# Mixer and MLP kernel: weight loads cut into fewer pieces, x8 to x10 moved in the load queue, tile groups and engine assignments redrawn

## Chip, cores and metric

The kernel runs on one core of a Trainium2 chip. The metric is the device time of one execution in microseconds (us), taken as the median of several runs. TensorE is called PE below, VectorE DVE, ScalarE ACT, GpSimd POOL and SyncE SP.

## What is computed

The input x has 2048 rows of 512 features in bf16. Two blocks follow each other, each with a residual addition. The first normalises the rows, multiplies by w1 (512 x 512), applies GELU, shifts the four quarters of the features by +1, -1, +2 and -2 rows, and multiplies by w2 (512 x 512). The second normalises again, multiplies by w3 (512 x 1792), applies GELU and multiplies by w4 (1792 x 512).

```python
h = _gelu(_layernorm(x, axis=-1) @ w1)
c = D // 4
g0 = jnp.pad(h[:, :, 0*c:1*c], ((0, 0), (1, 0), (0, 0)))[:, :S, :]
...
hs = jnp.concatenate([g0, g1, g2, g3], axis=-1) @ w2
x1 = x + hs
h2 = _gelu(_layernorm(x1, axis=-1) @ w3) @ w4
return x1 + h2
```

## The kernel before

**Tiles and stages.** The 2048 rows are 16 tiles of 128 rows. All weights and all of x stay in SBUF. A tile t goes through these steps, and their names are used below. A tile index q from 0 to 15 means layer 1 of tile q; q from 16 to 31 means layer 2 of tile q - 16.

- `dma_x` loads x rows (L369), `dma_w` loads weight chunks (L378). One load can cover several tiles or chunks.
- `ln` makes the statistics and the normalised rows xn. Statistics are made by DVE (`bnst`, `bnag`: L415, L417), or, for the indices in `STAT_ACT`, by ACT (`sum` L394, `ssq` L399) with small DVE operations (`mean`, `msq`, `vpe`). POOL computes `rstd` with a power (L422). The normalisation `norm` runs on DVE (L443), ACT (L452) or POOL (L455), as `NORM` says; on ACT and POOL it needs one more small value, `nmr`, from DVE or POOL (`NMR`). Tile 0 is only centred, in two halves (L433), and its `rstd` is applied in its GELU.
- The transposition of xn to xT is either a DMA transpose that SP issues (`tp`, L461) or four PE transposes (`sa`, `sb`, `ty` in the script, L488), with a copy out of PSUM by ACT, DVE or both (`EVAC`, L496).
- `up1` multiplies by w1 (L624; tile 0 alone in another layout, `rows0`, L526, with the transposition `th` back), `mix` by w2 with shifted rows (L664), `up2` by w3 (L624), `down` by w4 (L693). GELU runs on ACT (L639). DVE adds the residuals: `x1` (L671, L675) behind `mix`, `res` (L701) behind `down`. Then SP writes the rows out (L704).

`up1` and `up2` work on groups of 1, 2 or 4 tiles (`GROUPS`): a group of n tiles gives matmuls of 128n columns. `mix` of tile t needs h of the next tile's first two rows as well, and so the group that holds them. `up2` needs all of w3, `down` all of w4.

**What sets the order.** PE's order is written out in `SCRIPT`. SP's and ACT's load order is written out in `LOADS`: an item such as `x7-10` is one load, `w3p`, `w3q`, `w3r`, `w3s` are the four quarters of a weight, `a` and `b` its halves, a bare name the whole; `@act` lets ACT issue it. An entry such as `tp6` says at which place in SP's list the transpose of that index stands; for an index that PE transposes it has no effect. The order of all else is planned when the program is built: `Program.order` gives every operation a due time counted from the PE order, and `Program.place` runs a list of operations through estimated durations, taking on each engine the ready operation that is due first. The planned order is fixed in the program; each engine works through its own list in that order and waits on semaphores, one per engine and one per DMA. `DUE`, `BEGIN` and `BIAS` are parameters of this plan. `emit` puts the waits: an operation that needs several loads carries one wait for each.

PSUM has two banks that `mix`, `down` and `th` take in turn (`next_bank`) and three pairs of banks that transposes and `up` take in turn (`next_pair`).

**The start.** PE first runs warm-up matmuls on zeros (`warm:11`, L717). Then come the transposes of tiles 0, 1 and 2, `rows0` for tile 0, `up1` for tiles 1 to 5 one by one, `mix` 0 to 3, and between them the transposes of tiles 3 to 5 and of layer 2's tiles 16 and 17. Behind them starts `up2:0`, the w3 product of tiles 0 and 1. It is the first operation that reads w3.

Of the kernel before, what the change touches and what calls it, by code (L numbers as in the profile page):

```python
# [25 lines left out]
class Program:  # L26
# [2 lines left out]

    HOP = {"pe": 200.0, "dve": 155.0, "act": 220.0, "pool": 120.0, "sp": 70.0}  # L30
    LOOK = {"dve": 300.0, "act": 300.0}
    DUE = 198048.0
    BEGIN = {"sp": 30.0, "act": 560.0, "pe": 400.0, "dve": 150.0, "pool": 450.0}
    ENTRY = 1900.0
    COLD, RESTART = 4300.0, 800.0
    LAG = {"load": 750, "tp": 700}
# [15 lines left out]
    def order(self):  # L52
# [58 lines left out]
        assert seen == len(self.ops), "cycle"  # L111
        if self.DUE:

            topo, left = [], [len(d) for d in preds]
            stack = [i for i, n in enumerate(left) if n == 0]
            while stack:
                i = stack.pop()
                topo.append(i)
                for j in succs[i]:
                    left[j] -= 1  # L120
                    if left[j] == 0:
                        stack.append(j)
            due, t = {}, self.DUE
            for op in self.ops:
# [12 lines left out]
        for op in self.ops:  # L137
            op.prio += BIAS.get(op.name, 0.0)
            if op.first is not None:
# [11 lines left out]
    def place(self, succs, order_only):  # L151
# [4 lines left out]
        for op in self.ops:  # L156
            if npend[op.idx] == 0:
                cands[op.eng].append(op)
        free = dict(self.BEGIN)
        rings = {"sp": [], "act": []}  # L160
# [96 lines left out]
        self.seq = out  # L257
        return out

GROUPS = {1: (1, 1, 1, 1, 1, 1, 2, 4, 2, 2), 2: (2, 4, 4, 4, 2)}  # L260
NORM = {1: "act", 5: "act", 6: "pool", 7: "pool", 8: "act", 9: "act", 10: "act", 11: "pool", 13: "pool", 18: "pool", 20: "pool", 21: "pool", 24: "act", 27: "pool", 28: "pool", 29: "pool"}
EVAC = {0: "dve", 1: "both", 4: "both", 5: "both", 6: "dve", 7: "dve", 8: "both", 9: "both", 10: "dve", 11: "both", 15: "both", 17: "dve", 19: "both", 20: "dve", 21: "dve", 24: "both", 25: "both", 29: "dve", 30: "both", 31: "dve"}
STAT_ACT = (0, 6, 7, 8, 9, 12, 13, 18, 21, 22, 25, 27)
TAIL = (256, 128, 128)
NMR = {0: "pool", 2: "pool", 3: "pool", 4: "pool", 5: "pool", 6: "pool", 7: "pool", 8: "pool", 14: "pool", 16: "pool", 18: "pool", 22: "pool", 25: "pool", 26: "pool", 28: "pool", 31: "pool"}
NAT = (0,)
SPLIT = (0,)
CSPLIT = ()
HEV = {0: "dve", 1: "dve", 2: "dve", 4: "dve", 6: "dve"}
BIAS = {"msq0": -366.448}  # L270
LOADS = """
x1 x2 w1a w1s w1r x3 x4 w2b x0@act w2q w2p x5 x6 tp5 w3r w3s x7-10 tp4 w3p tp5 w3q w4q w4p tp16 x12 w4r x11
w4s tp7 x13-14 x15
"""
SCRIPT = """
warm:11 sa:0 sb:0 ty:1-2 ra:0 rb:0 up1:1 th:0 up1:2 mix:0 ty:3 mix:1 ty:4 up1:3-4 ty:5 mix:2 ty:16 mix:3
ty:17 up1:5 up2:0 mix:4 down:0 up1:6 down:1 up1:7 mix:5-6 up1:9 mix:10 mix:9 up1:8 mix:8 mix:7 up2:1 mix:11
mix:13 up2:2 mix:12 down:5 down:2-3 mix:15 up2:3 mix:14 down:6 down:13 down:9 up2:4 down:4 down:10 down:7
down:11 down:8 down:12 down:14-15
"""  # L280

def bass_standalone__mixer_s_mlp__prompt_kernel(nc, x, w1, w2, w3, w4, out):
# [3 lines left out]
    NT, DC, FC = S // P, D // P, F // P  # L286
    groups = {l: [(sum(GROUPS[l][:i]), n) for i, n in enumerate(GROUPS[l])] for l in GROUPS}
    NXN, NO, NPAIR, NOB, NJ = 16, 4, 3, 2, 4
# [8 lines left out]
    with ExitStack() as es:  # L297
# [87 lines left out]
        def ln(layer, t):  # L385
# [3 lines left out]
            col = lambda a: a[:, q : q + 1]  # L389
            if q in STAT_ACT:  # L390
                if layer == 1:
# [22 lines left out]
            else:  # L414
# [4 lines left out]
                       writes=[(("mv", q), 0), (("vpe", q), 0)], dur=75)  # L419
            var = vpe[:, q : q + 1] if q in STAT_ACT else mv[:, q, 1:2]  # L420
            pg.add("pool", f"rstd{q}",
                   lambda e: e.tensor_tensor(col(rstd), var, neghalf[:], ALU.pow),  # L422
                   reads=[(("vpe", q), 0), (("neghalf",), 0)], writes=[(("rstd", q), 0)], dur=470)
            how = NORM.get(q, "dve")
            dst = xn_buf[:, slot(q), :]
# [19 lines left out]
            else:  # L445
                eng = NMR.get(q, "dve")
                pg.add(eng, f"nmr{q}",
# [17 lines left out]
        def pe_transpose(t, q, pair):  # L465
            layer = 1 if q < NT else 2
            how = EVAC.get(q, "act")
            if pair:
# [104 lines left out]
        def h_transpose(t):  # L573
            g = group_of[1, t]
            how = HEV.get(t, "act")
            k = NAT.index(t)
# [71 lines left out]
        def mm_mix(t):  # L648
# [20 lines left out]
            wr = [(("x1", t), 0)]  # L669
            if NT + t in STAT_ACT:  # L670
                f = lambda e: e.scalar_tensor_tensor(x1_sb[:, t, :], dst, 1.0, x_sb[:, t, :], ALU.mult, ALU.add,  # L671
# [197 lines left out]
```

## Time and profile before

| what | value |
|---|---|
| median of 5 runs | 137.07 us (136.97 to 137.83) |
| the profiled execution's own time | 136.99 us |
| its span, first to last instruction | 135.2 us |
| granted PE clock | 1.000 |
| PE's first useful matmul | 4.77 us |
| DMA moved in the slices up to 17 us | 158 to 378 GB/s |
| loads: x 2 MB; w1, w2 0.5 MB each; w3, w4 1.75 MB each | 26 issues (25 on SP, 1 on ACT) |

All times inside the span are counted from its start. Two further things help in reading the profile. A wait for several semaphores is put down to the one that seems to have come last, so that a wait for a load can carry the name of a compute engine. And a matmul's shown length holds its way through the array; the distance from one start to the next is what it costs PE.

### The profile page before, as it was taken

To read this page: it belongs to the slowest core of one execution; us is meant where nothing else is said; L and a number is where in the kernel's file an instruction comes from. 1 tells how busy PE (TensorE), PEld (TensorE's weight loads), DVE (VectorE), ACT (ScalarE), POOL (GpSimd) and SP (SyncE) were. 2 spreads that over 40 slices of the span, in tenths; PEclk is the share of its full clock that TensorE was granted. 3 is DMA by queue.
4 is the path that set the end of the run, shared out by engine and by line. 5 is a ranking of instruction groups with operands and counts; after the bars stand their busy time and mean duration, and the time that the engine had idled before them with its cause. 6 is when DMAs were issued, how large, how long until landed. Compare 5 with 4: busy or idle time off the path is not lost.

```text
span 135.2 us, 2020 instructions
## 1 busy us (share of the span) xinstructions
PE 131.0 (97%) x779; PEld 71.7 (53%) x791; DVE 52.2 (39%) x143; ACT 57.5 (43%) x92; POOL 27.7 (20%) x60
## 2 busy tenths in 40 slices
PE   8999799999999999999999999999999999999994
PEld 3478588464466444444444444444446854444463
DVE  3889785784168820070005325002502202214222
ACT  6679889970675376655550003566000640000000
POOL 2434497259042310025003001000100000000000
DMA  5899999944543033001100311100030101111112
GB/s 158 290 305 378 378 346 204 161 66 95 112 121 63 19 79 76 0 0 39 39 5 0 78 39 39 39 0 0 4 81 18 59 0 39 39 44 39 39 39 78
DMA packets 21449, 12.19 MB, mean 90 GB/s; under 512 B 14016, under 2 KB 20928, under 8 KB 21440
## 3 DMA queue, kind: packets, MB, share of 16 engines
q1 hardware_dynamic: 20864, 11.80, 33.3%
q10 hardware_dynamic: 576, 0.26, 0.7%
q8 instruction: 6, 0.10, 0.3%
q14 instruction: 3, 0.02, 0.0%
HBM read 6.82 MB, written 2.10 MB: 66 GB/s over the span
## 4 chain that ended last, share of the span: by engine, by line
PE 84%; DMA 6%; SPq 3%; ACT 2%; DVE 1%; issue 1%; DVEq 0%
PE y_ps L624 41%; PE o_ps L693 36%; PE o_ps L664 8%; DMA x_sb<-in_x_dram 6%; SPq L378 2%; SPq L369 1%; ACT junk L399 1%; ACT junk L394 1%; DVE x_sb L671 1%; DVE x_sb L675 0%; ACT xnT L496 0%; DVE vpe L411 0%; DVE o_sb L701 0%; DVEq L818 0%
## 5 line engine op out<-in xcount | busy, mean ns | idle before, releaser
L624 PE MATMUL y_ps<-xnT,w_sb 128*128 128x512 bf16 (+2 forms) x420 | 63.6, 308 | 1.2 <-DVE x_sb L675 1.0
L624 PEld LDWEIGHTS y_ps<-xnT,w_sb 128*128 128x128 bf16 x424 | 38.3, 98 | 25.7 <-DVE x_sb L675 1.1
L693 PE MATMUL o_ps<-w_sb,h2T 128*128 128x512 bf16 (+2 forms) x248 | 48.9, 355 | 0.2
L639 ACT ACTIVATE h2T<-y_ps 128x1024 bf16<-128x1024 f32 (+1 forms) x29 | 28.6, 994 | 39.8 <-PE y_ps L624 39.6
L693 PEld LDWEIGHTS o_ps<-w_sb,h2T 128*128 128x128 bf16 x252 | 23.4, 98 | 24.9 <-issue 0.4
L701 DVE TENSOR_TENSOR o_sb<-o_ps,x_sb 128x512 bf16<-128x512 f32 (+2 forms) x18 | 11.3, 630 | 35.5 <-PE o_ps L693 30.5
L422 POOL TENSOR_TENSOR rstd<-mv,neghalf 128x1 f32<-128x1 f32 x20 | 11.2, 560 | 44.1 <-DVE mv L417 43.7
L675 DVE TENSOR_TENSOR x_sb<-o_ps,x_sb 128x512 bf16<-128x512 f32 x11 | 7.5, 684 | 22.1 <-PE o_ps L664 22.1
L664 PE MATMUL o_ps<-w_sb,hT 128*128 128x512 bf16 x60 | 14.9, 379 | 0.2
L415 DVE BATCH_NORM_STATS2 st<-x_sb 128x6 f32<-128x512 bf16 x20 | 13.6, 684 | 2.4 <-DMA x_sb<-in_x_dram 2.2
L422 POOL TENSOR_TENSOR rstd<-vpe,neghalf 128x1 f32<-128x1 f32 x12 | 6.6, 552 | 22.5 <-DVE vpe L411 17.7
L639 ACT ACTIVATE hT<-y_ps 128x512 bf16<-128x512 f32 (+1 forms) x10 | 8.1, 809 | 6.6 <-PE y_ps L624 6.4
L664 PEld LDWEIGHTS o_ps<-w_sb,hT 128*128 128x128 bf16 x64 | 6.1, 98 | 6.0
L399 ACT ACTIVATE junk<-x_sb 128x512 bf16<-128x512 bf16 x12 | 7.5, 624 | 2.7 <-DVE x_sb L671 2.6
L443 DVE TENSOR_SCALAR xn_buf<-x_sb,mv,rstd 128x512 bf16<-128x512 bf16 x15 | 6.6, 441 | 4.2 <-POOL rstd L422 3.2
L671 DVE SCALAR_TENSOR_TENSOR x_sb<-o_ps,x_sb 128x512 bf16<-128x512 f32 x5 | 3.4, 689 | 12.2 <-PE o_ps L664 12.2
L455 POOL TENSOR_SCALAR xn_buf<-x_sb,rstd,nmr 128x512 bf16<-128x512 bf16 x10 | 7.6, 768 | 1.0 <-DVE nmr L448 0.4
L452 ACT ACTIVATE xn_buf<-x_sb,nmr,rstd 128x512 bf16<-128x512 bf16 x6 | 4.8, 810 | 0.9 <-DVE mv L417 0.9
L717 PE MATMUL o_ps<-zeros 128*128 128x512 bf16 x11 | 4.3, 570 | 0.6 <-POOLq L854 0.6
L394 ACT ACTIVATE junk<-x_sb 128x512 bf16<-128x512 bf16 x7 | 4.4, 623 | 1.3 <-DMA x_sb<-in_x_dram 1.3
L417 DVE BATCH_NORM_AGGREGATE mv<-st 128x2 f32<-128x9 f32 x20 | 3.8, 191 | 0.3
L488 PE MATMUL y_ps<-ident,xn_buf 128*128 128x128 bf16 x32 | 3.0, 220 | 0.1
(34 smaller groups left out, 27.9 us busy)
## 6 DMA issues: line engine op xcount, KB each, us to landing
out_dram<-o_sb SPq DMA_DIRECT2D x15, 128.0 KB, 1.7
w_sb<-in_w_dram SPq DMA_DIRECT2D x4, 448.0 KB, 7.5
x_sb<-in_x_dram SPq DMA_DIRECT2D x9, 128.0 KB, 3.7
w_sb<-in_w_dram SPq DMA_DIRECT2D x2, 512.0 KB, 8.8
w_sb<-in_w_dram SPq DMA_DIRECT2D x2, 384.0 KB, 9.2
w_sb<-in_w_dram SPq DMA_DIRECT2D x2, 256.0 KB, 4.0
w_sb<-in_w_dram SPq DMA_DIRECT2D x4, 128.0 KB, 3.8
x_sb<-in_x_dram SPq DMA_DIRECT2D x1, 512.0 KB, 7.7
```

Source lines behind the costliest of these rows:

```text
L394: (lambda d: (lambda e: e.activation(d, src, ACT_F.Copy, scale=1.0 / D, accum_out=mv[:, q, 0:1])))(junk[:, b, :]),
L399: (lambda d: (lambda e: e.activation(d, src, ACT_F.Square, accum_out=sums[:, q, 1:2])))(junk[:, b, :]),
L415: pg.add("dve", f"bnst{q}", lambda e: e.bn_stats(st9[:, q, 0:6], src), reads=rs, writes=[(("st", q), 0)], dur=605)
L422: lambda e: e.tensor_tensor(col(rstd), var, neghalf[:], ALU.pow),
L443: lambda e: e.tensor_scalar(dst, src, mv[:, q, 0:1], rstd[:, q : q + 1], ALU.subtract, ALU.mult),
L455: f = lambda e: e.tensor_scalar(dst, src, rstd[:, q : q + 1], nmr[:, q : q + 1], ALU.mult, ALU.add)
L624: ins = e.matmul(y_ps[:, p, W * i : W * (i + 1)], wsb[:, dc, P * fc : P * (fc + 1)], src[:, dc, P * t0 : P * t0 + W], start=(dc == 0), sto ...
L639: (lambda d, s: (lambda e: e.activation(d, s, ACT_F.Gelu_apprx_tanh)))(dst, ysrc),
L664: ins = e.matmul(dst, hT[:, j, c0 : c0 + P], w2_sb[:, j, :], start=(j == 0), stop=(j == DC - 1))
L675: f = lambda e: e.tensor_tensor(x1_sb[:, t, :], dst, x_sb[:, t, :], ALU.add)
L693: ins = e.matmul(dst, h2T[:, fc, P * t : P * (t + 1)], w4_sb[:, fc, cs], start=(fc == 0), stop=(fc == FC - 1))
L701: (lambda d, c: (lambda e: e.tensor_tensor(o_sb[:, oi, c], d, x1_sb[:, t, c], ALU.add)))(dst, cs),
```

## The change

Loads. w1 comes in two halves (before: a half and two quarters), w2 in two halves (before: a half and two quarters), w3 in one load (before: four quarters), w4 in two halves (before: four quarters). x4 and x5 come as one load, x6 and x7 as one, x8 to x10 as one, x11 and x12 as one. x8 to x10 stand behind w4's first half; before, x7 to x10 stood between two halves of w3. `tp6` is issued ahead of x11 to x15.

Groups. Layer 1 has groups of tiles 0, 1, 2, 3, 4-5, 6, 7-10, 11-12, 13-14, 15 (before: 0, 1, 2, 3, 4, 5, 6-7, 8-11, 12-13, 14-15). Layer 2 has 0-1, 2-5, 6-9, 10-11, 12-15 (before: 0-1, 2-5, 6-9, 10-13, 14-15).

PE's order. Up to `up2:0` the same tiles are worked, with one warm-up matmul less and some transposes moved. From there on, `up1:5` (tile 6) and both downs of tiles 0 and 1 come before `mix:5`, and later `mix`, `up2` and `down` steps are in another order.

Engines. The centring of tile 0 moves from DVE to POOL, the norm of tile 1 from ACT to DVE, that of tile 3 from DVE to ACT, that of tile 5 from ACT to DVE, that of index 16 from DVE to POOL; other norms, statistics and PSUM copies move likewise. The plan's parameters change too, and with them the planned order on DVE, ACT and POOL.

```diff
-    DUE = 198048.0
-    BEGIN = {"sp": 30.0, "act": 560.0, "pe": 400.0, "dve": 150.0, "pool": 450.0}
+    DUE = 164483.0
+    BEGIN = {"sp": 30.0, "act": 150.0, "pe": 400.0, "dve": 150.0, "pool": 450.0}
...
-GROUPS = {1: (1, 1, 1, 1, 1, 1, 2, 4, 2, 2), 2: (2, 4, 4, 4, 2)}
-NORM = {1: "act", 5: "act", 6: "pool", 7: "pool", 8: "act", 9: "act", 10: "act", 11: "pool", 13: "pool", 18: "pool", 20: "pool", 21: "pool", 24: "act", 27: "pool", 28: "pool", 29: "pool"}
...
-STAT_ACT = (0, 6, 7, 8, 9, 12, 13, 18, 21, 22, 25, 27)
+GROUPS = {1: (1, 1, 1, 1, 2, 1, 4, 2, 2, 1), 2: (2, 4, 4, 2, 4)}
+NORM = {0: "pool", 3: "act", 7: "pool", 8: "act", 9: "pool", 10: "pool", 11: "pool", 12: "pool", 14: "act", 15: "act", 16: "pool", 18: "act", 19: "act", 24: "pool", 25: "act", 26: "pool", 27: "pool", 29: "pool", 30: "pool", 31: "act"}
...
+STAT_ACT = (0, 7, 9, 12, 13, 15, 18, 21, 25, 29, 30)
...
-HEV = {0: "dve", 1: "dve", 2: "dve", 4: "dve", 6: "dve"}
-BIAS = {"msq0": -366.448}
+HEV = {0: "dve", 4: "dve"}
+BIAS = {}
 LOADS = """
-x1 x2 w1a w1s w1r x3 x4 w2b x0@act w2q w2p x5 x6 tp5 w3r w3s x7-10 tp4 w3p tp5 w3q w4q w4p tp16 x12 w4r x11
-w4s tp7 x13-14 x15
+x1 x2 tp2 x0@act w1a w1b x3 x4-5 tp5 w2a w2b x6-7 w3 tp17 w4a x8-10 w4b tp6 x11-12 tp1 tp16 x13-15
 """
 SCRIPT = """
-warm:11 sa:0 sb:0 ty:1-2 ra:0 rb:0 up1:1 th:0 up1:2 mix:0 ty:3 mix:1 ty:4 up1:3-4 ty:5 mix:2 ty:16 mix:3
-ty:17 up1:5 up2:0 mix:4 down:0 up1:6 down:1 up1:7 mix:5-6 up1:9 mix:10 mix:9 up1:8 mix:8 mix:7 up2:1 mix:11
-mix:13 up2:2 mix:12 down:5 down:2-3 mix:15 up2:3 mix:14 down:6 down:13 down:9 up2:4 down:4 down:10 down:7
-down:11 down:8 down:12 down:14-15
+warm:10 sa:0 sb:0 ty:1 ra:0 rb:0 ty:2 up1:1 th:0 up1:2 mix:0 ty:3 ty:5 mix:1 ty:4 up1:3-4 ty:16 mix:2 ty:17
+mix:3 up2:0 mix:4 up1:5 down:1 down:0 mix:5 up1:6-7 mix:8 mix:6 up1:9 mix:9-10 up1:8 mix:7 mix:11 up2:1
+mix:13 mix:15 up2:3 down:5 mix:12 up2:2 mix:14 down:2 down:4 down:3 down:6-8 down:11 down:9 up2:4 down:10
+down:12-15
 """
```

`EVAC` (which engine copies a PE transpose out of PSUM) and `NMR` change too. Of the transposes that PE makes, 0 goes from DVE to ACT and DVE by halves, 2 from ACT to both, 5 from both to ACT, and 16 from ACT to DVE; 1, 3, 4 and 17 stay as they were.

## The prediction, made before the changed kernel ran

> **What bounds the kernel now.** I read the busy shares first, then the chain that ended last, the waits of TensorE (PE), three stretches of the span, and last the single DMA issues and instructions around the one gap.
>
> The shares (engine, busy us, share of the span, instructions):
> ```profile
> PE 131.0 (97%) x779; PEld 71.7 (53%) x791; DVE 52.2 (39%) x143; ACT 57.5 (43%) x92; POOL 27.7 (20%) x60
> ```
> PE is the bound; only its gaps and its start can be won. The stretches (from:to, length, busy us of each engine, clock, DMA share, GB/s) are: from PE's first useful matmul to its gap, the gap, and the rest.
> ```profile
> 4.77:16.20 11.43, 11.20 (x135) 8.43 (x135) 9.67 (x31) 9.48 (x24) 4.00 (x9) 1.00 1.01 346
> 16.20:17.17 0.97, 0.02 (x2) 0.03 (x2) 0.79 (x3) 0.97 (x4) 0.91 (x3) 1.00 1.09 353
> 17.17:133.40 116.23, 115.66 (x634) 61.71 (x644) 39.10 (x102) 44.52 (x63) 20.94 (x37) 1.00 0.26 60
> ```
> I count the third stretch by hand. PE's pitch is 216 ns for 512 columns (down0: 14 in 3.02 us), 109 ns for 256 (16 in 1.75), 59 ns for 128 (16 in 0.94) and 0.22 us for four transposes. Summed from 17.17 over the script, I reach 44.13 exactly where up2:1 starts and 133.3 at the end: **behind 17.17 nothing is left to win.** In the first stretch the sum is 11.03 us of 11.43, so 0.4 us are small waits. The large one is the gap:
> ```profile
> PE y_ps L624 <- DVE x_sb L675: 1.0, 1, 1.0
> ```
> ```profile
> 17.17 6.27 PE y_ps L624 x56
> ```
> The first line (waits) names DVE's x1 addition, the second (chain) the work behind the gap, up2:0. But up2:0 reads only xT of tiles 16 and 17, whose last copy out of PSUM (DVE, 15.45) ended at 15.86, and w3. So the named engine is not the cause. The issue of w3's second quarter (start, us) and its landing (last number, us after the start):
> ```profile
> 7.79 1.05 SPq L378 DMA_DIRECT2D w_sb<-in_w_dram  x1
> ```
> ```profile
> w_sb<-in_w_dram SPq DMA_DIRECT2D x1, 448.0 KB, 9.0
> ```
> 7.79 + 9.0 = 16.79: **the gap waits for w3's last quarter.** The remaining 0.35 us is the waiting itself: up2:0 carries six semaphore waits (four loads, ACT, DVE), 0.06 us each. PE's idle 0.38 us "issue" before down0 (also six) and 0.19 before rows0's second half (three) give the same price.
>
> **The change, part by part.**
> *PE work.* The same tiles are transposed by PE (0 to 5, 16, 17), and matmul counts by width agree. Ahead of up2:0, tiles 4 and 5 become one group of 256 columns (1.75 us in place of 2 x 0.94, -0.13); behind it tiles 6 and 15 become single groups where 6-7 was one (+0.13). Sum 0, but the end is then the start of up2:0 + 116.2 + 0.13, if no new wait appears.
> *w3's place in the queue.* Before, w3's last byte stands behind 4224 KB (x 0 to 10, w1, w2, w3), after behind 3840 KB, since x8 to x10 (384 KB) go behind w4's first half. The four-tile x load took 14.44 - 12.98 = 1.46 us of landing time per 512 KB, so 384 KB are 1.1 us: w3 lands at 16.79 - 1.1 = 15.7. Fewer, larger issues at the start might fill the engines earlier (DMA share 0.67 in us 3 to 4): 0 to 0.4 us better. [...]landings ran from 1.0 us behind the moved bytes (x6) to 2.0 (w3), so at worst 16.6. I take 15.7. Up2:0 then has two waits in place of six: 0.12 us, not 0.35. So w3 frees PE at about 15.8, and **the chain ahead of up2:0 becomes the limit.**
> *The start.* Tile 0's centring moves from DVE to POOL in halves. No 256-wide POOL row exists; POOL's 512-wide norm took 768 ns, its 128x1 TENSOR_SCALAR 262, so by the line between them 515 (ends 0.26, DVE's own time, and 0.77). Behind rstd1 (ends 4.04) the halves end at 4.55 and 5.07, where DVE ended at 4.57 and 4.75. Norm1 goes from ACT (5.22) to DVE, at 4.07. Here a rule speaks against the change: the Trainium skill, SBUF — State Buffer, section "Who interferes with whom", says that a DVE tensor_scalar in a two-port mode and a POOL instruction hold one port pair, and the later one waits for the whole of the other. The trace has one such meeting:
> ```profile
> 30.79 0.77 POOL L455 TENSOR_SCALAR xn_buf<-x_sb,rstd,nmr 128x512 bf16<-128x512 bf16 x1
> 30.84 0.87 DVE L443 TENSOR_SCALAR xn_buf<-x_sb,mv,rstd 128x512 bf16<-128x512 bf16 x1 [0.30 <-POOL rstd L422]
> ```
> DVE's 0.87 (median of that line: 0.41) ended 0.15 behind POOL. By the row norm1 ends 0.15 behind one half (4.70) or both (5.2); by the rule, with a whole DVE turn between the halves, the second half ends near 5.5 and its transposes start at 5.6. Without any meeting they start at 5.2. I take +0.25 (0 to 0.45).
> *Walking PE on.* With pitches from the trace (bn_stats 0.61, with its own aggregate behind it 0.72, DVE norm 0.33, 256-wide copy 0.19, x1 add 0.65, POOL rstd 0.55, nmr 0.26, GELU 0.60 and 1.02, ACT sum with readout 0.72, PE to DVE or ACT 0.2) and no meeting: rows0 ends 6.37, ty2, up1:1 at 6.60 (6.67 before), up1:2 7.77, mix0 8.75, ty3 9.6, ty5 9.83 (norm5 ready 9.54), mix1 10.05, ty4 10.98 (norm4 ends 10.83), up1:3 11.2, up1:4 12.14, ty16 13.89 (norm16 on POOL: 13.43), mix2 14.1, ty17 15.0 (norm17 14.43), mix3 15.2 (its GELU ends 15.09), up2:0 16.07. Most inputs are ready 0.05 to 0.5 us before PE asks, so the moves of norms, copies and statistics between DVE, ACT and POOL cost nothing here, and the cover is that thin. With +0.25 and 0.1 for touches, **up2:0 starts at 16.4** (16.1 to 16.9).
> *Queues passed.* w2b's landing (behind 1792 KB, as x5 before: 5.0 + 3.8 = 8.7) meets mix0 at 8.75 to 9.0. On ACT, sum7 stands ahead of the copies of ty3 and ty5 and waits for x6-7 (x6 at 9.2 before, now 128 KB more: 9.7); the copy for up1:3 ends at 11.0, PE asks at 11.2. In SP's queue w4b is issued by about 14, as 2.0 MB stay outstanding there; tp6 follows when norm6 is done (15.1), then x11 to x15, then tp7 to tp11.
> *Behind up2:0.* Before, tp6 landed at 18.42 + 4.7 = 23.1, 0.6 us behind w4's last quarter (14.40 + 8.1 = 22.5); here issue and landing of each in turn:
> ```profile
> 18.42 1.30 SPq L461 DMA_TRANSPOSE xnT<-xn_buf  x1
> ```
> ```profile
> xnT<-xn_buf SPq DMA_TRANSPOSE x1, 4.7
> ```
> ```profile
> 14.40 0.43 SPq L378 DMA_DIRECT2D w_sb<-in_w_dram  x1
> ```
> ```profile
> w_sb<-in_w_dram SPq DMA_DIRECT2D x1, 512.0 KB, 8.1
> ```
> After, w4 ends behind 6016 KB in place of 6272: about 21.9, tp6 22.5. Up1:5 (tile 6) is asked for at 16.4 + 6.13 + 0.86 = 23.4: 0.9 us of cover; down1 follows at 24.4. x8 to x10 land at about 19.2 (5120 KB; before, w4p at the same place: 9.6 + 9.8); sums, norms and the transposes of tiles 7 to 10 (SP takes 1.3 us each, 2.5 to land) end near 29, up1:6 starts at 31.2. tp21 lands near 41.5, up2:1 starts at 43.8. I cost these moves at nothing; later orders stand behind 3 us per down.
> *One warm-up matmul less.* It ends 4.3 in place of 4.5; transposes start at 4.7 as before. The Trainium skill, TensorE: Matmul & The Clock Gate, section "Part 1: The HAM clock gate", puts the full clock after about 3.4 us of sustained work. Warm-up weight loads here go from 0.43 apart to 0.31 at 4.03 to 4.34, so it comes under the tenth matmul: cost 0 by the row; if it slips past the now idle 0.3 us, by the rule up to 3.4 us at half rate, 1.7 us. I take 0.
>
> **Sum.** 17.17 - 16.4 = 0.77, less 0.13: 0.64 us. The profiled execution took 136.99 us (span 135.2 and 1.8 around it), 0.08 below the median of 137.07. 136.99 - 0.64 = 136.35, and with the median's 0.08, **136.4 us** (-0.5%). 0.5%, 0.69 us, is about what a measurement of this kernel can tell from no change.
>
> **The rivals.**
> *The gap is refilled ahead of up2:0* (31%): x6-7 lands at 10.5, so sum7 holds the copy for up1:3 until 11.8, 0.6 us late; or both POOL halves run late; or w3 lands at 16.6. Up2:0 starts at 16.8 to 17.2: about 136.9. For it: DVE was busy 9.67 of 11.43 us there, and covers are thin. Against: 384 KB are off w3's way.
> *The transpose of tile 6 lands late* (13%): it now stands directly behind 2.7 MB of w3, x8-10 and w4 in one queue. The price is us for us from 23.4; past a landing at 24.0 the gain is gone, past 24.8 it is slower by over 0.5%. At 25.0, 136.4 + 1.6 = 138.0. Against: 256 KB less stand before it than before.
> *The change doesn't do what it says* would be w3 landing no earlier (16.8): up2:0 at 16.9, 136.9, inside the first rival.
>
> **Chances.** Main case 56%: 136.0 to 136.8. Over 0.5% faster means under 136.38: most of the lower half and the walk without a meeting (136.1), 46%. Within 0.5%: 39%. Slower: 15%, the late transpose or a missed clock. The range runs from 135.9 to 137.5.
>
> **What would show it.** Right: up2:0 starts near 16.4 with under 0.3 us of wait; w3 lands by 16; transposes of tile 0's second half start at 5.2 to 5.6; from up2:0 to the end 116.3 us. Wrong: a PE wait before up1:5, up1:6 or up2:1, a weight load pitch of 0.43 beyond 4.3, or up1:3 held by ACT's copy of tile 3.

## The result and the profile after

The changed kernel takes **136.13 us** in the median (43 runs; the middle half lies from 136.07 to 136.16), the kernel before 136.97 us beside it (80 runs; the middle half from 136.50 to 137.46). The ratio is 0.9942 with a 95% interval of 0.9928 to 0.9956, so 0.58% faster. Not only the median moved: between the quartiles the runs of before are spread ten times as wide. Some runs of either kernel are slow ones, over 1.5% above its fastest (five of the changed kernel's, two of these at 200.06 and 233.68 us), and the ratios, their intervals and the spans given for experiments leave slow runs out, so that a ratio is not exactly the quotient of the two medians. The profiled execution of the changed kernel took 136.20 us, with a span of 134.9 us.

In the changed kernel every line number is one lower than before. First its busy shares:

```profile
PE 131.0 (97%) x777; PEld 71.5 (53%) x790; DVE 50.8 (38%) x134; ACT 57.6 (43%) x90; POOL 31.5 (23%) x70
```

PE's work is the same; POOL took over 3.8 us of work. The stretches show where the idle time lies now. They run from the span's start to PE's first useful matmul, from there to `up2:0`, and from `up2:0` to the end (columns as before):

```profile
0.00:5.16 5.16, 4.45 (x10) 1.34 (x10) 2.63 (x8) 2.82 (x6) 2.52 (x15) 1.00 0.56 176
5.16:16.85 11.69, 10.97 (x118) 8.12 (x121) 9.85 (x28) 7.71 (x16) 6.46 (x12) 1.00 1.07 376
16.85:133.10 116.25, 115.58 (x650) 62.05 (x659) 38.11 (x100) 47.10 (x68) 22.56 (x44) 1.00 0.26 59
```

Before, PE had 11.43 us of walk and a gap of 0.97 us up to `up2:0`; now it has a walk of 11.69 us and no gap, but it starts 0.39 us later (5.16 against 4.77). The last stretch is as long as it was. PE's only wait among useful work has changed its place:

```profile
PE y_ps L487 <- POOL xn_buf L432: 0.6, 1, 0.6
```

L487 is PE's transpose and L432 the centring of tile 0: PE waits once, for 0.6 us, for POOL's second half. No wait stands before `up2:0`, as the timeline of PE has it (start, length):

```profile
16.85 6.28 PE L623 MATMUL y_ps<-xnT,w_sb 128*128 128x256 bf16 x56
```

w3 had long been there. Its one load was issued at 4.52 us, and landed 9.3 us later, at 13.8 us (before: 16.8):

```profile
4.52 0.47 SPq L377 DMA_DIRECT2D w_sb<-in_w_dram  x1
```
```profile
w_sb<-in_w_dram SPq DMA_DIRECT2D x1, 1792.0 KB, 9.3
```

Landings differ from one execution to the next: eight others with w3 at this place of the list (a1, a3, c2, d1, g, g2, h1, h2 below) had it at 14.2 to 14.5 us, and with the list of before it was there at 16.4 to 16.8 (before, a2, a4). So the gap that bounded the start is gone by a margin of 2 to 3 us, and a new wait ahead of it gave back a part. The timeline of the changed kernel around that wait:

```profile
4.18 1.82 POOL L432 TENSOR_SCALAR xn_buf<-x_sb,mv 128x256 bf16<-128x256 bf16 x2
4.23 0.57 DVE L442 TENSOR_SCALAR xn_buf<-x_sb,mv,rstd 128x512 bf16<-128x512 bf16 x1
...
5.16 0.28 PE L487 MATMUL y_ps<-ident,xn_buf 128*128 128x128 bf16 x2
```

The two halves of the centring take POOL 1.82 us together, 0.92 each, and the transposes of the second half start at 6.06 us.

**The span and what lies around it.** Every run has a time and a span, and their difference is time that no trace shows. In the changed kernel it is 1.26 to 1.39 us in all of its runs. In the kernel before (67 runs beside the experiments b1, b2, c2 and g) it has two values: 1.27 to 1.38 us in 25 runs, 1.62 to 1.92 us in 42, and nothing between; the spans of the two sets are alike (medians 135.2 and 135.3). The median span of before is 135.1 to 135.4 us on the chips of the experiments, that of after 134.8 us in its own runs. So of the 0.84 us between the medians about 0.4 us are inside the span, and about 0.4 us (1.75 to 1.31) outside it. Only on the third chip of the experiments do both kernels have spans side by side: there 0.7 us are inside (135.4 to 134.7, h1), again with about 0.4 outside. The experiments are therefore read by both.

### The profile page after: what moved, and what is told of

It is laid out like the page before. It is cut to its first block, busy times and chain, and to the rows that moved or that the text cites. A ratio compares the mean times of both kernels' runs of the same rounds, so it can differ in the third digit from the quotient of the medians.

```text
span 134.9 us, 2004 instructions
## 1 busy us (share of the span) xinstructions
PE 131.0 (97%) x777; PEld 71.5 (53%) x790; DVE 50.8 (38%) x134; ACT 57.6 (43%) x90; POOL 31.5 (23%) x70
## 4 chain that ended last, share of the span: by engine, by line
PE 94%; DMA 2%; POOL 1%; issue 1%; DVE 1%; SPq 0%
PE y_ps L623 46%; PE o_ps L692 36%; PE o_ps L663 10%; DMA x_sb<-in_x_dram 2%; PE y_ps L487 1%; POOL xn_buf L432 1%; PE y_ps L525 1%; DVE st L414 1%; DVE o_sb L700 0%; PE o_ps L591 0%; DVE mv L416 0%; POOL rstd L421 0%; SPq L853 0%
## 5 line engine op out<-in xcount | busy, mean ns | idle before, releaser
L414 DVE BATCH_NORM_STATS2 st<-x_sb 128x6 f32<-128x512 bf16 x21 | 14.1, 678 | 2.8 <-DMA x_sb<-in_x_dram 2.6
L663 PE MATMUL o_ps<-w_sb,hT 128*128 128x512 bf16 x59 | 14.9, 379 | 0.3
L421 POOL TENSOR_TENSOR rstd<-vpe,neghalf 128x1 f32<-128x1 f32 x11 | 6.0, 549 | 28.5 <-DVE vpe L410 28.5
L454 POOL TENSOR_SCALAR xn_buf<-x_sb,rstd,nmr 128x512 bf16<-128x512 bf16 x11 | 8.4, 768 | 0.8 <-DVE nmr L447 0.4
L398 ACT ACTIVATE junk<-x_sb 128x512 bf16<-128x512 bf16 x11 | 6.9, 624 | 2.2 <-DVE x_sb L670 2.2
L442 DVE TENSOR_SCALAR xn_buf<-x_sb,mv,rstd 128x512 bf16<-128x512 bf16 x12 | 5.5, 455 | 2.8 <-POOL rstd L421 2.6
L451 ACT ACTIVATE xn_buf<-x_sb,nmr,rstd 128x512 bf16<-128x512 bf16 x8 | 6.3, 806 | 0.6 <-POOL nmr L447 0.6
L393 ACT ACTIVATE junk<-x_sb 128x512 bf16<-128x512 bf16 x6 | 3.7, 624 | 0.8 <-DMA x_sb<-in_x_dram 0.8
L487 PEld LDWEIGHTS y_ps<-ident,xn_buf 128*128 128x128 bf16 x32 | 2.1, 98 | 2.9 <-POOL xn_buf L432 1.8
```

Source lines behind the costliest of these rows:

```text
L398: (lambda d: (lambda e: e.activation(d, src, ACT_F.Square, accum_out=sums[:, q, 1:2])))(junk[:, b, :]),
L414: pg.add("dve", f"bnst{q}", lambda e: e.bn_stats(st9[:, q, 0:6], src), reads=rs, writes=[(("st", q), 0)], dur=605)
L442: lambda e: e.tensor_scalar(dst, src, mv[:, q, 0:1], rstd[:, q : q + 1], ALU.subtract, ALU.mult),
L451: f = lambda e: e.activation(dst, src, ACT_F.Identity, bias=nmr[:, q : q + 1], scale=rstd[:, q : q + 1])
L454: f = lambda e: e.tensor_scalar(dst, src, rstd[:, q : q + 1], nmr[:, q : q + 1], ALU.mult, ALU.add)
L663: ins = e.matmul(dst, hT[:, j, c0 : c0 + P], w2_sb[:, j, :], start=(j == 0), stop=(j == DC - 1))
```

## The experiments

My theory was the prediction's: w3 no longer holds PE, and the start holds it instead. The rival readings were that the load list alone makes the gain, that the groups and PE's order make it, or that the start costs nothing because it is absorbed further on. All medians stand beside runs of the kernel before on the same chip. The last two columns are medians too. An experiment has 6 to 22 runs (a2, a4 and g2 have 6).

| run | time | ratio to before | interval | span | around it |
|---|---|---|---|---|---|
| before, on three chips | 136.79 to 137.08 | 1 | | 135.1 to 135.4 | 1.68 to 1.75 |
| after | 136.13 | 0.9942 | 0.9928 to 0.9956 | 134.8 | 1.31 |
| a1: before, new loads | 137.38 | 1.0022 | 0.9999 to 1.0046 | 136.05 | 1.31 |
| a2: after, old loads | 138.00 | 1.0112 | 1.0073 to 1.0151 | 136.1 | 1.85 |
| a3: after, DVE centres | 135.84 | 0.9935 | 0.9913 to 0.9957 | 134.5 | 1.33 |
| a4: before, POOL centres | 137.96 | 1.0118 | 1.0070 to 1.0166 | 136.2 | 1.79 |
| b1: after, w3 in quarters | 136.10 | 0.9962 | 0.9943 to 0.9981 | 134.7 | 1.35 |
| b2: after, x8 to x10 early | 136.12 | 0.9945 | 0.9928 to 0.9962 | 134.8 | 1.32 |
| c2: before, new loads fitted | 136.46 | 0.9986 | 0.9962 to 1.0011 | 134.9 | 1.56 |
| g: after, POOL subtract and mult | 136.56 | 0.9998 | 0.9970 to 1.0026 | 135.2 | 1.31 |
| h1: after again | 136.05 | 0.9939 | 0.9914 to 0.9964 | 134.7 | 1.33 |
| h2: DVE centres again | 135.92 | 0.9923 | 0.9892 to 0.9953 | 134.6 | 1.31 |
| d1: DVE centres, ty3 before mix0 | 135.89 | 0.9900 | 0.9871 to 0.9930 | 134.6 | 1.31 |
| g2: POOL mult and add | 135.66 | 0.9902 | 0.9863 to 0.9941 | 134.3 | 1.31 |

a1 to a4 ran on one chip, b1, b2, c2 and g on a second, h1, h2, d1 and g2 on a third. Each edit makes the planner place everything anew, so some operations on DVE, ACT and POOL also change places: none in b1 and g2, a dozen in a3, some tens in a1, a2, b2 and c2.

### a1: the kernel before with the changed load list

```diff
-x1 x2 w1a w1s w1r x3 x4 w2b x0@act w2q w2p x5 x6 tp5 w3r w3s x7-10 tp4 w3p tp5 w3q w4q w4p tp16 x12 w4r x11
-w4s tp7 x13-14 x15
+x1 x2 tp2 x0@act w1a w1b x3 x4-5 tp5 w2a w2b x6-7 w3 tp17 w4a x8-10 w4b tp6 x11-12 tp1 tp16 x13-15
```

> The kernel before with the changed load list alone (groups, PE order and engine assignments stay; the plan's order on DVE, ACT, POOL and SP follows the new arrivals). Theory (the load order is what closed the gap): w3 lands near 14, up2:0 starts near 16.2 in place of 17.17, no wait before it, about 0.9 us faster, ratio 0.993. Rival (the gain is from the new PE order and engine assignments): ratio 0.998 or more.

It took 137.38 us: the time did not fall, and the span grew by 0.9 us. The gap at `up2:0` is gone (it starts near 16.7 us), and PE's waits show two others:

```profile
PE y_ps L623 <- issue: 1.2, 1, 1.2
PE o_ps L663 <- ACT hT L638: 0.8, 1, 0.8
```

The first stands before `up1:7`, the group of tiles 8 to 11. In the new list tile 11 comes with x12 behind w4's second half and lands at 22.2 us. The transposes of the four tiles then leave SP one after the other, the last two in this line (start, length, two issues), and a transpose needs 2.5 us to land:

```profile
29.01 2.58 SPq L460 DMA_TRANSPOSE xnT<-xn_buf  x2
```

The last is issued at 30.32 and lands at 32.8, where PE asks at 31.7. "issue" in the wait line thus hides a DMA. The second wait is before `mix:0`. The ACT operation that it names is the GELU of tile 2, which `mix:0` doesn't read and which ended at 9.52 us, when PE was already loading `mix:0`'s weights (9.41). w2's second half landed at 3.49 + 5.7 = 9.2 us. So the load list does remove the gap, but it brings two others. One comes from its fit to the old groups (tile 11). The other comes from the list itself: w2 was complete at 8.3 us in the profile of before and at 9.2 here.

### a2: the changed kernel with the load list of before

The diff is that of a1 with the signs exchanged.

> The changed kernel with the load list of before alone. Theory: w3's last quarter lands near 16.8 again and its six waits follow, up2:0 starts near 17.15 behind a gap of 0.3 us (PE is ready at 16.85), so about the time of before, ratio 1.000, and none of the 0.8 us that the start lost shows. Rival: the loads do not matter, ratio 0.994 as changed.

138.00 us: slower, not the same. PE's waits name tile 5's norm:

```profile
PE y_ps L488 <- DVE xn_buf L443: 0.9, 1, 0.9
```

The changed order asks for the transposes of tile 5 before those of tile 4. In the old list x5 stands alone behind w2 and lands at 8.6 us; DVE's timeline shows tile 5's statistics and its norm late behind it:

```profile
9.46 0.65 DVE L415 BATCH_NORM_STATS2 st<-x_sb 128x6 f32<-128x512 bf16 x1
...
11.42 0.40 DVE L443 TENSOR_SCALAR xn_buf<-x_sb,mv,rstd 128x512 bf16<-128x512 bf16 x1
```

`up2:0` starts at 18.22 us, though w3's last quarter was there at 16.4. Some 0.2 us of this belong to the profiled execution: PE was still at half its later pace until 6.6 us, and `up1:1` started at 7.71 (7.50 in the changed kernel). The rival that the new order is good by itself falls, as the rival that the new loads are good by themselves fell in a1. In span, each alone costs about 1.0 us, and both together save 0.3 to 0.7.

### c2: the kernel before with the new loads, fitted to its groups

a1's wait before `up1:7` comes from tile 11. So tile 11 goes with x8 to x10, as the old group of four wants it.

```diff
-x1 x2 tp2 x0@act w1a w1b x3 x4-5 tp5 w2a w2b x6-7 w3 tp17 w4a x8-10 w4b tp6 x11-12 tp1 tp16 x13-15
+x1 x2 tp2 x0@act w1a w1b x3 x4-5 tp5 w2a w2b x6-7 w3 tp17 w4a x8-11 w4b tp6 x12 tp1 tp16 x13-15
```

(the first line is a1's list)

> The kernel before with the changed load list, but x8 to x11 as one load and x12 alone, so that its group of tiles 8 to 11 has all its rows behind w4's first half. With the list as changed, that group waited 1.2 us for tile 11 before up1:7. Theory (loads and tile groups have to fit each other): that wait goes, up2:0 starts near 16.7 as there, ratio 0.994 to 0.997. Rival (the wait before up1:7 has another cause, such as the order of SP's transposes): it stays, ratio 1.002.

The wait is gone: `up1:7` starts without one, at 31.62, and of PE's waits among useful work only one of 0.3 us before `mix:0` is left.

```profile
31.62 3.62 PE L623 MATMUL y_ps<-xnT,w_sb 128*128 128x512 bf16 x15
```
```profile
PE o_ps L663 <- DVE mv L416: 0.3, 1, 0.3
```

Its median span, 134.9 us, is 0.25 us under that of before on the same chip (135.15) and within 0.2 us of b1's and b2's (134.7 and 134.8), which are the changed kernel but for a change in its loads. So by these medians a good half of the gain inside the span needs nothing but loads that fit, and the new groups, PE's new order and the engines add 0.1 to 0.2 us. In time c2 stays 0.3 us behind b1 and b2, since its time around the span is 1.56 us, not 1.32. Its ratio of 0.9986 misses the expected 0.994 to 0.997, and can't be told from no change.

### b1 and b2: which part of the load list brings w3 earlier

b1 gives the changed kernel w3 in four loads again, b2 puts x8 to x10 ahead of w3.

```diff
-... w2a w2b x6-7 w3 tp17 w4a x8-10 w4b ...
+... w2a w2b x6-7 w3r w3s w3p w3q tp17 w4a x8-10 w4b ...
```

> The changed kernel with w3 in four quarter loads at the same place of the list; all other order stays. In the profile of the changed kernel w3 landed at 13.8 and PE asked for it at 16.85. Theory (w3 now has some 3 us of slack; only the six waits of 0.06 us come back): last quarter lands by 15.8, up2:0 at 16.85 to 17.1, ratio 0.994 to 0.996. Rival (one load in place of four is what closed the gap): last quarter lands past 16.8, ratio 0.998 or more.

```diff
-... w2a w2b x6-7 w3 tp17 w4a x8-10 w4b ...
+... w2a w2b x6-7 x8-10 w3 tp17 w4a w4b ...
```

> The changed kernel with x8 to x10 ahead of w3 and not behind w4's first half. Theory: w3 lands 1.1 us later, near 15, still ahead of PE, so the move by itself is worth nothing while PE reaches up2:0 at 16.85: ratio 0.993 to 0.996, no wait before up2:0. Rival (the move is what closed the gap): a wait before up2:0, ratio 0.998 or more.

Neither moves the time (136.10 and 136.12 us). Issue and landing of the last quarter in b1:

```profile
6.13 0.43 SPq L377 DMA_DIRECT2D w_sb<-in_w_dram  x1
```
```profile
w_sb<-in_w_dram SPq DMA_DIRECT2D x1, 448.0 KB, 7.8
```

6.13 + 7.8 = 13.9 us, as the single load's 13.8: the number of w3's loads isn't what brought w3 forward. Nor did the waits for four loads, expected at 0.06 us each, cost anything that shows: the last matmul of `mix:3` started at 16.55 and `up2:0` at 16.76, one matmul's distance later. In b2, w3 as one load:

```profile
5.03 0.49 SPq L377 DMA_DIRECT2D w_sb<-in_w_dram  x1
```
```profile
w_sb<-in_w_dram SPq DMA_DIRECT2D x1, 1792.0 KB, 9.9
```

5.03 + 9.9 = 14.9 us. That is 1.1 us later than in the changed kernel's own profile, but only 0.4 to 0.8 us later than in the eight others. The prediction gave 1.1 us to 384 KB in the queue; at the 376 GB/s of the changed kernel's second stretch they are 1.05 us by estimate, and b2 agrees as far as one execution can tell. `up2:0` asks at 16.6, so even there w3 isn't late, and the move of x8 to x10 is worth nothing in this kernel. More than half of the 2 to 3 us comes from the rest of the list, since b2's w3 is still 1.5 to 1.9 us ahead of the 16.4 to 16.8 of the old list. By 13.5 us, 4.13 MB had been moved in the changed kernel against 3.82 MB before, which is 0.8 us of moving by estimate; the other part, how long w3 landed behind the moving of its bytes, was 2.0 us before and 0.9 to 1.8 in the executions of the changed list. Why was not isolated.

### a3 and a4: who centres tile 0

```diff
-NORM = {0: "pool", 3: "act", 7: "pool", ...
+NORM = {3: "act", 7: "pool", ...
```

> The changed kernel with tile 0's centring back on DVE alone. POOL took 0.92 us for each half where 0.515 was estimated. Theory (that delay lies on PE's path all the way to up2:0): the second half's transposes start near 4.9 in place of 6.06, up2:0 near 16.1 in place of 16.85, 0.7 us faster than the changed kernel, ratio to before 0.989. Rival (the delay is absorbed, as other inputs of the walk are late anyway): under 0.2 us, ratio 0.993 to 0.994.

```diff
-NORM = {1: "act", 5: "act", 6: "pool", ...
+NORM = {0: "pool", 1: "act", 5: "act", 6: "pool", ...
```

> The kernel before with tile 0's centring on POOL alone. Theory: the start comes 0.8 us later, but PE waits for w3 until 17.17 anyway, so up2:0 starts at 17.2 and the time stays, ratio 1.000 (at most 1.002). Rival (a late start shifts the end by itself): 0.8 us slower, ratio 1.006.

With DVE centring (a3), PE's transposes run on without a wait from 4.71 us and `up1:1` starts at 6.74 in place of 7.50. Then PE waits before `mix:0`:

```profile
PE o_ps L663 <- DVE st L414: 0.6, 1, 0.6
```

`mix:0` doesn't read those statistics. It reads h of tiles 0 and 1, which was complete at 8.60 us, and w2, whose second half landed at 3.48 + 5.6 = 9.1; `mix:0` started at 9.50. Of 0.76 us won at the start, 0.36 were left at `up2:0` (16.49 against 16.85), and 0.3 in the median span. The expected ratio of 0.989 was missed; 0.9935 is what the rival gave. In a4, POOL's centring costs the kernel before 1.2 us of waits, as its source line and PE's waits show:

```profile
L433 POOL TENSOR_SCALAR xn_buf<-x_sb,mv x2: 917/920/924, 5.2 to 6.1; 128x256 bf16<-128x256 bf16 x2
```
```profile
PE y_ps L488 <- POOL xn_buf L433: 1.2, 2, 0.6
```

Here POOL began at 5.2, behind another `rstd` in its list, `up1:1` started 1.8 us late, and `up2:0` about 1.0 us late: `up1:5`, directly before it, started at 17.2 us, and `up2:0` at 18.2. I had expected w3's gap to absorb all of it; the delay was larger than the gap. So a late start is absorbed only as far as the next load's landing lies behind it.

### g and g2: the price of POOL's centring

The sum of the prediction took 0.515 us for one half, and the trace has 0.92. Two runs change only the form of the operation, and g2 leaves every other operation in its place. g subtracts the mean and multiplies by 1. g2 lets ACT make the negative mean of tile 0 and has POOL multiply by 1 and add it; the values are the same.

```diff
-tensor_scalar(a, b, mv[:, q, 0:1], None, ALU.subtract)
+tensor_scalar(a, b, mv[:, q, 0:1], 1.0, ALU.subtract, ALU.mult)
```

> The changed kernel with tile 0's centring still on POOL in halves, but as subtract and multiply by 1.0 in one instruction, the shape of operations that POOL's other norms have. Same result. Theory (the instruction with one operation is slow on POOL by itself, 0.92 us for 256 columns against 0.77 for 512 with two): a half takes about 0.5 us, the second half's transposes start near 5.3, but w2's landing near 9.1 takes most of it back: ratio 0.9935 to 0.994. Rival (DVE, holding the shared port, or the narrower tile makes it slow): it stays at 0.92.

```diff
-activation(d, src, ACT_F.Copy, scale=1.0 / D,
+activation(d, src, ACT_F.Copy, scale=(-1.0 if q == 0 else 1.0) / D,
...
-tensor_scalar(a, b, mv[:, q, 0:1], None, ALU.subtract)
+tensor_scalar(a, b, 1.0, mv[:, q, 0:1], ALU.mult, ALU.add)
```

> The changed kernel with tile 0's mean kept with the other sign (ACT's scale is negative for tile 0), so that POOL's centring is a multiplication by 1.0 and an addition in place of a subtraction. Same result. Theory (subtracting is what is slow on POOL: 0.92 us alone and 1.14 with a multiplication, against 0.77 us for twice the columns with multiply and add): a half takes 0.5 us, its transposes start near 5.3, ratio 0.992. Rival (the half-wide tile is what is slow): 0.9 us or more, ratio 0.994 or above.

The source line of the centring in g, then in g2 (shortest, median and longest in ns):

```profile
L432 POOL TENSOR_SCALAR xn_buf<-x_sb,mv x2: 1140/1142/1145, 4.1 to 5.2; 128x256 bf16<-128x256 bf16 x2
```
```profile
L432 POOL TENSOR_SCALAR xn_buf<-x_sb,mv x2: 479/490/500, 3.9 to 4.3; 128x256 bf16<-128x256 bf16 x2
```

g falsified my first thought, that one operation alone is slow for want of a second: the second one adds 0.22 us, and the span is 0.4 to 0.5 us longer than b2's and b1's on the same chip. g2 shows that both forms with the subtraction are slow and multiply-add is fast on the same 256 columns. An addition or a multiplication alone was not run, so whether subtracting is the slow case or multiply-add a fast one stays open. The prediction's 0.515 was drawn from a multiply-add row, and was right for that and wrong for this operation. In g2 the second half's transposes start 1.02 us behind the end of the `rstd` before (3.87 to 4.89), in the changed kernel 1.88 us (4.18 to 6.06). PE's waits in g2 among useful work, and its `up2:0`:

```profile
PE y_ps L487 <- POOL xn_buf L432: 0.2, 1, 0.2
PE o_ps L663 <- DMA w_sb<-in_w_dram: 0.2, 1, 0.2
```
```profile
15.94 6.28 PE L623 MATMUL y_ps<-xnT,w_sb 128*128 128x256 bf16 x56
```

`up2:0` is 0.9 us earlier than in the changed kernel's profile, of which 0.3 are x1's earlier landing in this execution. By medians g2 is the fastest kernel of the study: 135.66 us, 0.4 below the changed kernel on the same chip (h1), and its span is 0.4 us shorter. Only 6 runs stand behind it, and the intervals of the two ratios overlap.

### h1, h2 and d1: the start once more, on one chip

h1 is the changed kernel as it is, h2 is a3's kernel again. d1 also has DVE centring, gives tile 3's norm to DVE and lets its transposes go before `mix:0`, to fill the wait for w2.

```diff
-NORM = {0: "pool", 3: "act", 7: "pool", ...
+NORM = {7: "pool", ...
...
-... up1:2 mix:0 ty:3 ty:5 mix:1 ...
+... up1:2 ty:3 mix:0 ty:5 mix:1 ...
```

> The changed kernel itself, on the chip of the next three, so that they can be compared with it: ratio 0.994, narrow spread, 136.1 us.

> The changed kernel with tile 0's centring on DVE, beside the changed kernel on one chip. Theory (0.76 us of start won, 0.4 to 0.56 of it given back at mix0, which waits for w2's second half near 9.2): 0.3 us faster than the changed kernel, ratio to before 0.992. Rival (absorbed entirely): ratio 0.994.

> As the last, and also tile 3's norm on DVE and its four transposes ahead of mix0, into the wait for w2. Theory: the wait before mix0 shrinks by the transposes' 0.22 us, up2:0 near 16.3, another 0.2 us, ratio 0.990 to 0.991. Rival (DVE, busy 10.2 of 11.8 us there, makes norm5, norm4 or norm17 late by as much): no gain or 0.2 us slower, ratio 0.992 to 0.994.

h1 took 136.05 us, h2 135.92, d1 135.89: no two of them can be told apart. In h2's profile `up1:1` started at 6.22 us, and the whole gain was gone at `mix:0`:

```profile
PE o_ps L663 <- DVE mv L416: 0.8, 1, 0.8
```

Again the engine named isn't the cause: h of tiles 0 and 1 was complete at 8.06 us, and w2's second half landed at 3.49 + 5.7 = 9.2, 0.2 us before PE took up `mix:0`. `up2:0` started at 16.63 in h1 and in h2. In d1 the wait before `mix:0` is gone, but in its profiled execution PE came to its full pace late. Its first eight transposes, and the same eight in a3:

```profile
4.89 1.06 PE L487 MATMUL y_ps<-ident,xn_buf 128*128 128x128 bf16 x8
```
```profile
4.71 0.61 PE L487 MATMUL y_ps<-ident,xn_buf 128*128 128x128 bf16 x8
```

They start 0.11 us apart in d1 and 0.06 in a3. They end 0.6 us later than in a3, more than the 0.22 us of transposes that the fill could win (`up2:0` at 16.90). What the fill is worth by itself stays open.

## Why the prediction was right, and where not

The forecast was 136.4 us (-0.5%), the measurement 136.13 (-0.58%), inside the range. The direction and the main mechanism held, two terms of the sum were off, and one part of the gain was not in the sum at all.

- **w3's landing** was given as 15.7 us and measured as 13.8 (14.2 to 14.5 in eight other executions). The term for 384 KB holds as far as b2 can tell (0.4 to 1.1 us), and the 0 to 0.4 us for fewer, larger issues was far too small (1.5 to 1.9 us for the rest of the list). It did no harm, since behind 16.1 us nothing more is to be had from w3. The rival "w3 no earlier" is out.
- **The start** was given +0.25 us (0 to 0.45) and took more. The failed step is "behind rstd1 the halves end at 4.55 and 5.07": 515 ns for a half, where the trace has 922. I drew the line through a multiply-add row and a tiny one, and took it that the operation's arithmetic makes no difference. The second half's transposes came at 6.06 and not at 5.2 to 5.6, and `up1:1` at 7.50 and not at 6.60 + 0.25. `rstd` itself also ended 0.14 us later (4.18 against 4.04) in this execution, as x1 had landed 0.15 us later.
- **The port rule.** The +0.25 us stood between the row of before and the Trainium skill's rule (SBUF — State Buffer, "Who interferes with whom": the later of two holders of the shared ports waits for the whole of the other). DVE's norm of tile 1 took 0.57 us here against its usual 0.41, and ended at 4.80, while POOL's first half ended at 5.10: it lost 0.16 us, but did not wait for the whole of POOL's operation. It took 0.57 us beside g's half of 1.14 us as well, and 0.58 beside g2's of 0.49: what DVE lost did not follow the length of POOL's operation, so that g2's norm, which ended 0.13 us behind POOL's half, doesn't speak for the rule either. Only the row of before, beside a 512-column multiply-add, comes near it. POOL lost nothing to DVE: both halves took the same 0.92 us, with DVE's norm beside the first only. So what delayed the start was POOL's own length, and not a meeting.
- **One warm-up matmul less** was given as free, with the full clock under the tenth matmul. The last warm-up matmuls (start, length together, number), first in the changed kernel, then in the kernel before:

```profile
3.59 1.49 PE L716 MATMUL o_ps<-zeros 128*128 128x512 bf16 x3
```
```profile
3.60 1.33 PE L717 MATMUL o_ps<-zeros 128*128 128x512 bf16 x4
```

  Before, these four started 0.43, 0.30 and 0.22 us apart; in the changed kernel the three started 0.43 apart to the last (4.01 and 4.44), so PE came to its full pace later than assumed. It cost nothing here, because PE had to wait for POOL's first half until 5.10 anyway, and the transposes at 5.16 then started 0.07 apart. The prediction's cost of 0 came out right for another reason.
- **The walk** from `up1:1` to `up2:0` was given as 16.07 - 6.60 = 9.47 us and measured as 16.85 - 7.50 = 9.35. So the pitches and the judgement that the moved norms, copies and statistics cost nothing held, for the walk as a whole. `up2:0` started at 16.85, in the range 16.1 to 16.9 but not at 16.4; other executions of the same PE order had 16.6 to 16.8 (h1, b1, b2).
- **Behind `up2:0`** I had added 0.13 us for two more single groups. The stretch measured 116.25 us, before 116.23. The term wasn't seen, and no run tests it alone.
- **Tile 6's transpose** landed at 16.14 + 6.0 = 22.1 us, as the timeline and the landing time of the changed kernel have it:

```profile
16.14 1.48 SPq L460 DMA_TRANSPOSE xnT<-xn_buf  x1
```
```profile
xnT<-xn_buf SPq DMA_TRANSPOSE x1, 6.0
```

  The prediction had 22.5; PE asked at 23.83. This rival did not come about. Its size was misstated: w3, x8 to x10 and w4 ahead of it are 3968 KB, 4.1 MB and not 2.7. The comparison with before (256 KB less) was right.
- **The rest of the time** is the step that the sum did not question: "span 135.2 and 1.8 around it" was carried over unchanged. The 1.8 became 1.3. In the profiles PE's gain is 17.17 - 16.85 = 0.32 us and the span's 0.3, half of the 0.64 predicted; the change around the span made up for the missing half. So the total is right by luck in that half: two errors of opposite sign cancelled.

What the runs show of that last part: it goes with the load list. With the list of before it is 1.68 to 1.85 us in the median whatever the rest (before, a2, a4). With the changed list, or b1's and b2's, it is 1.31 to 1.35 whatever the rest (a1 with the old groups, after, a3, b1, b2, g, h1, h2, d1, g2). Neither the number of w3's loads nor the place of x8 to x10 matters for it (b1, b2), but c2's list, one tile different from a1's, has 1.56. What happens in that time, and why the kernel before has two values of it, stays open.

The cause of the gain is thus settled only in its parts: in span, the gap before `up2:0` is gone because w3 lands earlier *and* groups and order fit what the loads bring (a1, a2, c2), less what POOL's slow subtraction costs (a3, g2). About 0.4 us more lies outside the span and follows the load list. Why the spread is narrower was not tested. Loads that are no longer on the path would narrow it; so would POOL's long centring, behind which PE waits until 6 us, whether its clock came early or late. The kernels with the new list and DVE's centring (a3, h2, d1) spread over 0.2 to 0.4 us between the quartiles, the changed kernel over 0.1.

## What to carry to other kernels

A load order and the order of the work that reads it are one decision: each of the two new halves alone made the span about 1 us longer, and the new list with one tile moved to suit the old groups (c2) did over half as much inside the span as the whole new plan. When a gap is removed, look for the next landing ahead of it on the same path: here w2's second half at `mix:0` took half of what a faster start won in a3 and all of it in h2, under the name of an engine that had nothing to do with it. Take a duration from a row with the same arithmetic, not only the same shape, and look at what lies around the span as well before carrying it over.

## What the runs showed of the hardware that was not expected

- **POOL's subtraction is slow beside its multiply-add.** For 128x256 bf16: subtract 922 ns, subtract and multiply 1142 ns, multiply and add 490 ns; multiply and add of 128x512 takes 768 ns. The Trainium skill, GPSIMD Engine Reference, section "3.1 Elementwise — side-by-side cycle accounting", states about 1.8 cycles for an element as the best case of a tight loop, 768 ns for 512 elements. That agrees with the multiply-add row of 512 columns; the subtract row takes 1.9 times as long as the multiply-add row on the same 256 columns.
- **DVE's loss beside POOL doesn't follow POOL's length.** The same norm took 0.57, 0.57 and 0.58 us beside POOL operations of 1.14, 0.92 and 0.49 us on 256 columns, and 0.41 alone.
- **Time outside the span goes with the program's load list**: 1.3, 1.56 or 1.75 us in the median, and two values in one and the same kernel.
- **Landings vary more than computing does.** w2's second half landed between 8.5 and 9.2 us in kernels whose list is the same up to it, and w3 between 13.8 and 14.5.
- **PE's full pace comes at very different times.** The starts of its matmuls halved their distance at about 3.5 us in a1, 4.3 in before and b2, 5.4 in c2, 6 in d1 and 6.7 in a2, while the first warm-up matmul started at 0.63 to 0.65 us in all of them. In a2, PE had waited in between. The clock that the profile's rows give is 1.00 throughout.
